# A gated-attention and soft-mixture kernel: PSUM halves as tiles of their own, halved first loads and y copies, and a new order of the first units and of the end

## Chip, cores and metric

One core of one Trainium2 chip runs the whole program. The metric is device time in microseconds (us) of one execution; lower is better. All data are fp32.

## The reference

For each of 4 batches and 8 heads a gated linear attention runs over 768 steps with head width 48; its output x (3072 rows of 384) goes through a soft mixture of 8 experts with 4 slots each.

```python
f = 1 / (1 + exp(-f_logit))
for t in range(768):
    state = f[:, :, t, :, None] * state + outer(k[:, :, t], v[:, :, t])
    y[:, :, t] = q[:, :, t] @ state
x = y as (3072, 384)
logits = x @ phi                                  # 3072 x 32
d = softmax of logits over the rows               # dispatch
slot_out[e] = relu((d.T @ x)[e] @ w1[e]) @ w2[e]  # 8 experts, hidden 1024
out = softmax of logits over the slots @ slot_out # combine
```

## The kernel before

**Units.** The sequence is cut into 6 chunks of 128 steps; a chunk of two batches is a unit (`u`, 12 units), with 16 (batch, head) pairs, two to a 128-partition block, in 8 blocks of 128 columns. For each unit the gates are turned into running sums by `d_exp`, `d_ln` (ScalarE) and `d_scan` (VectorE, line 191). `d_p` and `d_g` (ScalarE, lines 194 and 200) make the two exponentials of it, and `d_q` and `d_k` (lines 208 and 204, GpSimd but for unit 0) scale q and k with them. TensorE then makes the scores in two halves (`scores`, line 232), VectorE masks them (`s_mask`, line 235), TensorE transposes k (`kt`, copied by `kt_copy` on ScalarE), and y is summed in PSUM from the carried state (`inter`, line 272) and the masked scores (`intra`, line 281, two halves `w`). `kv` makes the unit's own contribution to the state, and `state_t` (line 257) and `state_2` (line 260), both on VectorE, carry it two units on. `y_copy` (ScalarE, line 293) takes y out of PSUM, `x_tr` transposes it back and `x_copy` takes one half out on ScalarE (line 311) and one on VectorE (line 313).

**Groups.** For each pair of units: `c_lg` (logits, line 325), `c_max`, `c_exp`, `c_tr` (transposes), `c_copy` (VectorE, line 353), `c_pin` (line 362) and `c_join` (VectorE, lines 366 and 367) keep the dispatch sum with a running maximum.

**End.** `up` (line 420, four times 24 matmuls), `turn` (line 426: transposes, then a masking multiply on VectorE), `down` (line 462, two column halves `h`), the combine softmax (`c_soft`, `c_soft2`, `c_ct`), `slot_out`, `slot_out2`, and for each half three `combine` and `store` steps, `flag` and `flag_2` compute a guard value that picks a slow path when the gates are too extreme (it does not run here).

**PSUM.** Four tiles of two banks each: `PA` holds the second scores half of unit 0, `x_tr`, `c_lg` and `c_pin`; `PB` holds y and `c_tr`; `PC` holds `kt` and `kv`; `PD` holds scores. Waits are set by the framework from the accesses to each tile.

**Order.** Every step is put on one list with a due time (`at`), unit `u` at `u * T` plus the offset of `OFF`; sorted, this gives each engine's program order, kept exactly. Units 0 and 1 have a list written out by hand. All loads and stores are issued by SyncE (SP), in the order of the list: the first loads in the list `first`, later ones by the offsets `lf`, `lk`, `lq`, `lv`, w1 and w2 pieces between them.

Of the kernel before, what the change touches and what calls it, by code (L numbers as in the profile page):

```python
# [31 lines left out]
def keep_order(tc):  # L32
# [16 lines left out]
    sc0=0, mask0=1.05, kt=1.1, ktok=1.95, sc1=2.85, mask1=3.95, inter=4.9, kv=5.4, intra0=5.7, st=6.2, s2=6.3, intra1=6.6, y=7.55,  # L49
# [8 lines left out]
def gla_soft_moe_kernel(ctx: ExitStack, tc: tile.TileContext, q, k, f, v, vd, phi, w1, w2, out):  # L58
# [65 lines left out]
    check = P([128, 8 * NU + NU + 2], "check")  # L124
# [12 lines left out]
    PA, PB, PC, PD = (pp.tile([128, 2, 512], F32, tag=n, name=n) for n in ("pa", "pb", "pc", "pd"))  # L137


    def consts_0():  # L140
        nc.gpsimd.memset(ones, 1.0)
        nc.vector.memset(again, 1.0)
        nc.vector.memset(again.rearrange("p (a t) -> p a t", t=L)[:, :, 0], 0.0)
        warm(20, PD[:, 1, :128])
        make_identity(nc, ident)
        nc.gpsimd.affine_select(mask, ones, pattern=[[1, L]], compare_op=ALU.is_ge, fill=0.0, base=0, channel_multiplier=-1)
        nc.vector.memset(PC, 0.0)
        nc.vector.memset(PB, 0.0)
# [73 lines left out]
    def SP(u, w):  # L222

        return PA if u == 0 and w else PD

    def scores(u, w):

        kq, qq = heads(R("k", u), L), heads(R("q", u), L)
        for p in range(4):
            for r in range(2):  # L230
                rs = slice(64 * r, 64 * r + D)
                nc.tensor.matmul(SP(u, w)[:, r, 128 * p : 128 * p + 128], kq[rs, 4 * w + p], qq[rs, 4 * w + p], start=True, stop=True)  # L232

    def s_mask(u, w):
        nc.vector.tensor_tensor(  # L235
            heads(R("sc", w), L), SP(u, w).rearrange("p r (a t) -> p (r a) t", t=L), mask.unsqueeze(1).broadcast_to([128, 8, L]), op=ALU.mult,
        )
# [25 lines left out]
    ys = heads(PB.rearrange("p w x -> p (w x)"), L)  # L263

    def inter(u):

        qq = heads(R("q", u), L)
        if u > 1:
            for p in range(4):
                for w, r in ((0, 0), (1, 1), (0, 1), (1, 0)):  # L270
                    a, o, rs = 4 * w + p, 64 * (r ^ w), slice(64 * r, 64 * r + D)
                    nc.tensor.matmul(  # L272
                        ys[o : o + D, a], heads(S0(u), D)[rs, a], qq[rs, a], start=p == 0, stop=False, skip_group_check=True,
                    )
# [22 lines left out]
    def y_last(u):  # L297
        t = xTs[u].rearrange("p n a t -> p n (a t)")
        nc.scalar.copy(t[:, 1, :256], PB[:, 1, :256])
        nc.vector.tensor_copy(t[:, 1, 256:], PB[:, 1, 256:])  # L300

    def x_tr(u):
        for w in range(2):
            for p in range(4):
                nc.tensor.transpose(PA[:, w, 128 * p : 128 * p + W], xTs[u][:W, w, p], ident[:W, :W])  # L305

    def x_copy(u, which=(0, 1)):
        x = xs[u].rearrange("p w (h d) -> p w h d", d=D)
        y = PA.rearrange("p w (h d) -> p w h d", d=64)[:, :, :, :D]
        if 0 in which:  # L310
            nc.scalar.copy(x[:, 0], y[:, 0])  # L311
        if 1 in which:
            nc.vector.tensor_copy(x[:, 1], y[:, 1])  # L313
# [41 lines left out]
    def pins(g):  # L355
        return PA[:, 1, :DM]
# [58 lines left out]
    UPB = [PA[:, 0], PA[:, 1], PC[:, 0], PC[:, 1]]  # L415
# [7 lines left out]
    def turn(j, hf):  # L423
        pt = PB[:, hf].rearrange("p (k m) -> p k m", k=4)
# [42 lines left out]
    def slot_out(h):  # L467
        hs_ = slice(HC * h, HC * h + HC)
        nc.vector.tensor_scalar(sob[:, hs_], PD[:, h, :HC], rzs, None, op0=ALU.mult)

    def slot_out2(h):

        hs_ = slice(HC * h, HC * h + HC)
        nc.tensor.matmul(PD[:, h, 256 : 256 + HC], same, sob[:, hs_], start=True, stop=True)
        nc.scalar.copy(s4[:, hs_], PD[:, h, 256 : 256 + HC])

    FIN = [[(PA, PC), (PB, PA), (PC, PB)], [(PA, PB), (PC, PD), (PA, PB)]]
    stage = [wr[:, 7 + 3 * h : 10 + 3 * h].rearrange("p a (n d) -> p (a n) d", d=HC).rearrange("p (v n) d -> p v n d", n=4) for h in range(NH)]

    def combine(h, y):  # L480

        hs_ = slice(HC * h, HC * h + HC)
        for x in range(2):
            for n in range(4):
                ns = slice(32 * n, 32 * n + 32)
                nc.tensor.matmul(FIN[h][y][n // 2][:, n % 2, HC * x : HC * x + HC], ct[ns, 2 * y + x], s4[ns, hs_], start=True, stop=True)
        for z in range(2):
            dst = stage[h][:, 2 * y : 2 * y + 2, 2 * z : 2 * z + 2].rearrange("p v n d -> p n v d")
            (nc.vector.tensor_copy if z else nc.scalar.copy)(dst, FIN[h][y][z][:, :, : 2 * HC].rearrange("p n (v d) -> p n v d", v=2))

# [244 lines left out]
```

## Time and profile before

| what | us |
|---|---|
| median of three runs | 175.89 (174.79 to 176.54) |
| the profiled execution, its own time | 177.31 |
| its span, first to last instruction | 175.6 |
| TensorE busy / VectorE / ScalarE / GpSimd | 145.7 / 105.1 / 91.7 / 54.5 |

A row of the timeline has the start in us, the duration in us, the engine (PE is TensorE, DVE VectorE, ACT ScalarE, POOL GpSimd, SPq SyncE's queue), the line, the operation, out and in tile, the shape and the number of instructions merged; in brackets stands the engine's idle time just before and what ended it. Releasers are inferred. TensorE's busy time contains pipelined work, and a slice of the page is a fortieth of the span, 4.39 us.

### The profile page before, as it was taken

The page shows a single profiled execution, that of the slowest core. Times are in us where ns is not written, and L with a number is a line of the kernel's source. Part 1 is how long each engine was busy: PE and PEld are TensorE (multiplying, and loading weights), DVE is VectorE, ACT ScalarE, POOL GpSimd, SP SyncE. Part 2 cuts the span into 40 slices and gives each one's busy share as a digit, 9 for nine tenths or more (in the row PEclk, how much of TensorE's full clock was granted, in tenths as well). Part 3 has the DMA queues.
Part 4 walks back from the last instruction along what each step waited for, and adds up shares of the span by engine and source line. Part 5 has one row for each costly group of instructions (what it writes and reads, how often), then busy time and mean ns, then how long its engine had stood idle before and what let it go on. Part 6 is the DMA issues. An engine that isn't in the chain of part 4 may idle for free.

```text
span 175.6 us, 5429 instructions
## 1 busy us (share of the span) xinstructions
PE 145.7 (83%) x2384; PEld 114.0 (65%) x2384; DVE 105.1 (60%) x143; ACT 91.7 (52%) x159; POOL 54.5 (31%) x43
## 2 busy tenths in 40 slices
PE   7679986799998989898989898999787997697600
PEld 7669875787886978697969786767422355464400
DVE  6786587629786959597859777581602327324600
ACT  4977794936868594949495865311311130223500
POOL 2007474741919091917372555400000000000000
PEclk9975999569999999999999999999999999999965
DMA  5999999969599999988899929999829990018790
GB/s 147 317 417 408 410 411 411 414 228 400 191 347 406 345 339 323 422 304 307 291 319 339 335 75 403 420 421 415 359 31 371 426 413 30 0 58 343 277 392 31
DMA packets 12848, 53.97 MB, mean 307 GB/s; under 512 B 1424, under 2 KB 1552, under 8 KB 12816
## 3 DMA queue, kind: packets, MB, share of 16 engines
q1 hardware_dynamic: 12816, 53.55, 79.5%
q8 instruction: 20, 0.33, 0.7%
q14 instruction: 12, 0.10, 0.2%
HBM read 48.82 MB, written 4.72 MB: 305 GB/s over the span
## 4 chain that ended last, share of the span: by engine, by line
PE 44%; DVE 28%; ACT 13%; issue 4%; DMA 4%; SPq 1%; DVEq 0%; ACTq 0%
DVE arena L191 11%; PE pb L272 6%; PE pc L250 5%; PE pd L462 4%; ACT arena L194 4%; DMA arena<-in_q_dram 4%; PE pd L232 4%; PE pa L420 3%; PE pc L420 3%; PE pa L325 3%; PE pa L362 3%; DVE arena L235 3%; PE pb L281 3%; DVE pc L257 3%; ACT arena L220 2%
## 5 line engine op out<-in xcount | busy, mean ns | idle before, releaser
L208 POOL TENSOR_TENSOR arena<-arena 128x1024 f32<-128x1024 f32 (+1 forms) x13 | 27.0, 2076 | 56.7 <-ACT arena L194 39.1
L232 PE MATMUL pd<-arena 48*128 48x128 f32 x368 | 27.7, 291 | 6.3 <-DVE arena L235 3.4
L235 DVE TENSOR_TENSOR arena<-pd,mask 128x1024 f32<-128x1024 f32 x23 | 27.8, 1210 | 4.0 <-PE pd L232 4.0
L191 DVE TENSOR_TENSOR_SCAN arena<-again,arena 128x1024 f32<-128x1024 f32 (+1 forms) x15 | 28.7, 1919 | 2.5 <-ACT arena L186 2.4
L232 PEld LDWEIGHTS pd<-arena 48*128 48x128 f32 x368 | 23.1, 193 | 10.6 <-DVE arena L235 5.5
L204 POOL TENSOR_TENSOR arena<-arena 128x1024 f32<-128x1024 f32 (+1 forms) x13 | 26.5, 2038 | 0.0
L281 PE MATMUL pb<-arena 128*48 128x128 f32 x384 | 24.4, 280 | 0.6 <-DVE arena L235 0.6
L281 PEld LDWEIGHTS pb<-arena 128*48 128x48 f32 x384 | 21.0, 126 | 1.6 <-DVE arena L235 0.9
L293 ACT COPY arena<-pb 128x1024 f32<-128x1024 f32 x11 | 11.1, 1011 | 14.5 <-PE pb L281 14.5
L194 ACT ACTIVATE arena<-arena 128x1024 f32<-128x1024 f32 (+1 forms) x15 | 13.3, 884 | 8.2 <-DVE arena L191 8.2
L183 ACT ACTIVATE arena<-arena 128x1024 f32<-128x1024 f32 (+1 forms) x14 | 13.1, 937 | 2.7 <-DMA arena<-in_f_dram 2.7
L272 PE MATMUL pb<-arena 48*48 48x128 f32 x320 | 11.8, 288 | 2.3 <-DVE el L353 2.3
L200 ACT ACTIVATE arena<-arena 128x1024 f32<-128x1024 f32 (+1 forms) x15 | 13.4, 892 | 0.3
L186 ACT ACTIVATE arena<-arena 128x1024 f32<-128x1024 f32 (+1 forms) x14 | 13.1, 936 | 0.4
L272 PEld LDWEIGHTS pb<-arena 48*48 48x48 f32 x320 | 9.1, 127 | 4.8 <-DVE el L353 2.9
L313 DVE COPY arena<-pa 128x384 f32<-128x384 f32 x12 | 6.6, 553 | 9.1 <-ACT arena L311 9.1
L427 DVE TENSOR_TENSOR arena<-pb,emask 128x512 f32<-128x512 f32 x4 | 2.8, 691 | 14.8 <-PE pb L426 14.8
L305 PE MATMUL pa<-ident,arena 112*128 112x112 f32 x96 | 11.3, 261 | 0.3 <-ACT arena L293 0.2
L217 PE MATMUL pc<-ident,arena 112*128 112x112 f32 x80 | 10.8, 280 | 0.5 <-POOL arena L204 0.5
L250 PEld LDWEIGHTS pc<-arena 128*48 128x48 f32 x320 | 9.1, 136 | 1.8 <-issue 1.7
L305 PEld LDWEIGHTS pa<-ident,arena 112*128 112x128 f32 x96 | 9.6, 141 | 0.8 <-ACT arena L293 0.6
L250 PE MATMUL pc<-arena 128*48 128x48 f32 x320 | 10.1, 221 | 0.0
(131 smaller groups left out, 201.4 us busy)
## 6 DMA issues: line engine op xcount, KB each, us to landing
wr<-in_w_dram SPq DMA_DIRECT2D x23, 768.0 KB, 8.6
arena<-in_w_dram SPq DMA_DIRECT2D x9, 768.0 KB, 8.0
arena<-in_k_dram SPq DMA_DIRECT2D x12, 512.0 KB, 6.4
arena<-in_q_dram SPq DMA_DIRECT2D x12, 512.0 KB, 7.2
arena<-in_f_dram SPq DMA_DIRECT2D x10, 512.0 KB, 7.0
arena<-in_v_dram SPq DMA_DIRECT2D x12, 384.0 KB, 7.3
out_dram<-wr SPq DMA_DIRECT2D x6, 768.0 KB, 4.2
arena<-in_f_dram SPq DMA_DIRECT2D x4, 256.0 KB, 5.1
```

Of the source, the lines that this page charges most:

```text
L183: nc.scalar.activation(cols(R("f", u), h), cols(R("f", u), h), AF.Exp, scale=-1.0, accum_out=a)
L191: nc.vector.tensor_tensor_scan(t, cols(again, h), t, 0.0, op0=ALU.mult, op1=ALU.add)
L194: nc.scalar.activation(cols(R("p", u), h), cols(R("f", u), h), AF.Exp, scale=-1.0)
L200: nc.scalar.activation(cols(G(u), h), cols(R("f", u), h), AF.Exp)
L204: (eng or nc.gpsimd).tensor_tensor(t, t, cols(G(u), h), op=ALU.mult)
L208: (eng or nc.gpsimd).tensor_tensor(t, t, cols(R("p", u), h), op=ALU.mult)
L232: nc.tensor.matmul(SP(u, w)[:, r, 128 * p : 128 * p + 128], kq[rs, 4 * w + p], qq[rs, 4 * w + p], start=True, stop=True)
L235: nc.vector.tensor_tensor(heads(R("sc", w), L), SP(u, w).rearrange("p r (a t) -> p (r a) t", t=L), mask.unsqueeze(1).broadcast_to([128, 8, ...
L250: nc.tensor.matmul(kvs[64 * r : 64 * r + D, a], kr[:, a, r], vb(u, a, r ^ a // 4), start=True, stop=True)
L272: nc.tensor.matmul(ys[o : o + D, a], heads(S0(u), D)[rs, a], qq[rs, a], start=p == 0, stop=False, skip_group_check=True,)
L281: nc.tensor.matmul(ys[o : o + D, 4 * w + p], vb(u, 4 * w + p, r ^ w), sc[:, r, p], start=u < 2 and p == 0, stop=p == 3, skip_group_check=True,
L305: nc.tensor.transpose(PA[:, w, 128 * p : 128 * p + W], xTs[u][:W, w, p], ident[:W, :W])
```

## The change

- **Tiles.** `PA` and `PB` become two tiles of one bank each (`PA[0]`, `PA[1]`, `PB[0]`, `PB[1]`); every user is rewritten to the bank it uses. `PC` and `PD` stay.
- **y in halves.** `y_copy` is two ScalarE copies of 128x512 (`y0` due after the first half of `intra`, `y1` after the second); for the last unit `y_last` (a split over ScalarE and VectorE) goes.
- **First loads.** k and q of unit 0 are loaded in column halves, q of unit 1 ahead of k, and v of unit 0 after both.
- **Order of units 0 to 3.** 28 instead of 20 `warm` matmuls (products of a tile of ones that nobody reads) before the first scores and 4 new ones before `kv` of unit 0; `s_mask` of unit 0 ahead of the scans of unit 1; second half of `d_q` of units 1 and 2 on VectorE; unit 2's gates partly in halves; `scan` of unit 3 after the first mask of unit 2 instead of ahead of it, `d_p` and `d_q` of unit 3 later.
- **End.** `up`, `turn`, `down`, `slot_out2`, `combine` get tiles of their own; `c_soft` moves ahead of the third `up`, `flag` into unit 11 and `flag_2` ahead of the fourth `up`; `combine` copies three tiles (one ScalarE copy of two banks, two VectorE copies of one).

```diff
-    PA, PB, PC, PD = (pp.tile([128, 2, 512], F32, tag=n, name=n) for n in ("pa", "pb", "pc", "pd"))
+    PA, PB = ([pp.tile([128, 512], F32, tag=f"{n}{w}", name=f"{n}{w}") for w in range(2)] for n in ("pa", "pb"))
+    PC, PD = (pp.tile([128, 2, 512], F32, tag=n, name=n) for n in ("pc", "pd"))
...
-        warm(20, PD[:, 1, :128])
+        warm(28, PD[:, 1, :128])
...
-    def y_copy(u):
-        t = xTs[u].rearrange("p n a t -> p n (a t)")
-        if u < NU - 1:
-            nc.scalar.copy(t, PB)
-        else:
-            nc.scalar.copy(t[:, 0], PB[:, 0])
+    def y_copy(u, which=(0, 1)):
+        for w in which:
+            nc.scalar.copy(xTs[u][:, w].rearrange("p a t -> p (a t)"), PB[w])
...
-    UPB = [PA[:, 0], PA[:, 1], PC[:, 0], PC[:, 1]]
+    UPB = [PA[0], PB[0], PA[0], PB[0]]
+    TURN = [[PB[1], PA[1]], [PB[1], PA[0]]]
+    DOWN = [PD[:, 0, :HC], PB[0][:, :HC]]
+    SUM = [PD[:, 1, 256 : 256 + HC], PA[0][:, 256 : 256 + HC]]
...
-    FIN = [[(PA, PC), (PB, PA), (PC, PB)], [(PA, PB), (PC, PD), (PA, PB)]]
+    FIN = [[(PC, PA[0], PA[1]), (PD, PB[1], PA[0]), (PC, PA[1], PB[1])], [(PC, PA[1], PB[1]), (PD, PA[0], PB[0]), (PC, PA[1], PB[1])]]
...
-        items = [(t_psi,), (c_exp, NV - 1, (1,)), (t_zs,), (up, 0, 0), (up, 0, 1), (c_tr, NV - 1, (1,)), (turn, 0, 0), (c_copy, NV - 1, (1,))]
-        items += [(up, 1, 0), (turn, 0, 1), (t_z,), (c_soft,), (up, 1, 1)]
+        items = [(t_psi,), (c_exp, NV - 1, (1,)), (t_zs,), (up, 0, 0), (up, 0, 1), (c_tr, NV - 1, (1,)), (c_copy, NV - 1, (1,)), (turn, 0, 0), (c_soft,)]
+        items += [(up, 1, 0), (turn, 0, 1), (t_z,), (flag_2,), (up, 1, 1)]
...
-    first = [(0, "f", 0), (0, "f", 1), (0, "k"), (0, "q"), (1, "f", 0), (1, "f", 1), (1, "k"), (0, "v"), (1, "q"), (2, "f"), (1, "v")]
+    first = [(0, "f", 0), (0, "f", 1), (0, "k", 0), (0, "q", 0), (0, "k", 1), (0, "q", 1), (1, "f", 0), (1, "f", 1), (1, "q"), (1, "k"), (0, "v"), (2, "f"), (1, "v")]
...
-        (d_exp, 1, 0), (d_ln, 1, 0), (d_exp, 1, 1), (d_ln, 1, 1), (d_pend, 0), (kt, 0), (d_scan, 1, 0), (s_mask, 0, 0), (d_p, 1, 0), (d_g, 1, 0),
-        (kt_copy, 0), (d_q, 1, 0), (d_k, 1, 0), (d_scan, 1, 1), (s_mask, 0, 1), (intra, 0, 0), (kv, 0), (d_p, 1, 1), (d_g, 1, 1), (d_q, 1, 1), (d_k, 1, 1),
-        (intra, 0, 1), (state_2, 0), (d_exp, 2), (y_copy, 0), (d_ln, 2), (d_pend, 1),
+        (d_exp, 1, 0), (d_ln, 1, 0), (d_exp, 1, 1), (d_ln, 1, 1), (d_pend, 0), (s_mask, 0, 0), (kt, 0), (d_scan, 1, 0), (d_scan, 1, 1), (s_mask, 0, 1),
+        (d_p, 1, 0), (d_g, 1, 0), (kt_copy, 0), (d_q, 1, 0), (d_k, 1, 0), (d_p, 1, 1), (d_g, 1, 1), (intra, 0, 0), (warm, 4, PD[:, 1, :128]), (kv, 0), (intra, 0, 1),
+        (d_q, 1, 1, V), (d_k, 1, 1), (state_2, 0), (d_exp, 2, 0), (d_ln, 2, 0), (y_copy, 0), (d_exp, 2, 1), (d_ln, 2, 1), (d_pend, 1),
...
-    for h in range(2):
-        for x, (fn, t) in enumerate(((d_scan, 1.5), (d_p, 2.9), (d_g, 3.0), (d_q, 2.95), (d_k, 3.05))):
-            at(T + t + 0.2 * h, fn, 2, h)
+    for t, fn, *args in (
+        (1.0, d_scan, 2, 0), (1.1, d_scan, 2, 1), (1.2, d_p, 2, 0), (1.25, d_g, 2, 0), (1.3, d_q, 2, 0), (1.35, d_k, 2, 0),
+        (2.0, d_p, 2, 1), (2.05, d_g, 2, 1), (2.1, d_k, 2, 1), (4.0, d_q, 2, 1, V),
+    ):
+        at(T + t, fn, *args)
+    early = {(1, "kv"): T + 6.0, (3, "scan"): 2 * T + 1.08, (3, "p"): 2 * T + 2.9, (3, "dq"): 2 * T + 2.95}
...
+    at((NU - 1) * T + 6.5, flag)
```

## Rows read from the trace of the kernel before

**Rows 1.** The page's slices: granted clock and DMA busy share, in tenths.

```profile
PEclk9975999569999999999999999999999999999965
DMA  5999999969599999988899929999829990018790
```

**Rows 2.** Timeline, the first 17 us.

```profile
1.06 6.23 PE L153 MATMUL pd<-ones 128*128 128x128 f32 x40 [1.06 <-POOL ones L141]
...
9.31 0.69 DVE L208 TENSOR_TENSOR arena<-arena 128x512 f32<-128x512 f32 x1 [0.57 <-DMA arena<-in_q_dram]
...
11.26 2.08 PE L232 MATMUL pa<-arena 48*128 48x128 f32 x16
...
14.22 1.63 POOL L208 TENSOR_TENSOR arena<-arena 128x512 f32<-128x512 f32 x1 [12.46 <-DMA arena<-in_q_dram]
...
14.96 1.95 PE L281 MATMUL pb<-arena 128*48 128x128 f32 x16
```

**Rows 3.** Timeline, 26 to 45 us, units 2 and 3.

```profile
26.24 1.16 PE L232 MATMUL pd<-arena 48*128 48x128 f32 x16
27.11 1.26 POOL L204 TENSOR_TENSOR arena<-arena 128x512 f32<-128x512 f32 x1
...
27.25 3.26 DVE L191 TENSOR_TENSOR_SCAN arena<-again,arena 128x1024 f32<-128x1024 f32 x1 [1.62 <-ACT arena L186]
...
30.44 1.19 DVE L235 TENSOR_TENSOR arena<-pd,mask 128x1024 f32<-128x1024 f32 x1
30.61 1.06 ACT L194 ACTIVATE arena<-arena 128x1024 f32<-128x1024 f32 x1 [2.49 <-DVE arena L191]
...
31.69 2.08 PE L232 MATMUL pd<-arena 48*128 48x128 f32 x16 [1.90 <-DVE arena L235]
...
39.88 2.28 DVE L191 TENSOR_TENSOR_SCAN arena<-again,arena 128x1024 f32<-128x1024 f32 x1
...
44.28 1.16 PE L232 MATMUL pd<-arena 48*128 48x128 f32 x16 [0.77 <-DVE arena L235]
```

**Rows 4.** Timeline of the loop, an even unit, in which a group ends.

```profile
71.38 0.56 DVE L313 COPY arena<-pa 128x384 f32<-128x384 f32 x1 [1.13 <-ACT arena L311]
...
71.99 0.85 PE L362 MATMUL pa<-arena,el 128*32 128x384 f32 x8 [0.53 <-DVE arena L313]
...
72.69 2.37 POOL L204 TENSOR_TENSOR arena<-arena 128x1024 f32<-128x1024 f32 x1
...
74.31 0.76 DVE L367 SCALAR_TENSOR_TENSOR sms<-sms,small 128x1 f32<-128x1 f32 x1
...
75.64 0.57 DVE L257 TENSOR_TENSOR pc<-pc,arena 128x384 f32<-128x384 f32 x1 [0.17 <-PE pc L250]
```

**Rows 5.** Timeline of the loop, a unit between two such.

```profile
100.60 1.09 PE L272 MATMUL pb<-arena 48*48 48x128 f32 x32 [0.76 <-DVE el L353]
100.95 2.38 POOL L204 TENSOR_TENSOR arena<-arena 128x1024 f32<-128x1024 f32 x1
...
103.67 2.28 DVE L191 TENSOR_TENSOR_SCAN arena<-again,arena 128x1024 f32<-128x1024 f32 x1
```

**Rows 6.** Timeline from the last unit to the last stores.

```profile
121.43 0.42 DVE L300 COPY arena<-pb 128x256 f32<-128x256 f32 x1 [3.05 <-ACT arena L299]
...
130.89 2.78 PE L420 MATMUL pa<-wr,et 128*32 128x512 f32 x24 [0.79 <-ACT arena L421]
...
135.41 2.78 PE L420 MATMUL pc<-wr,et 128*32 128x512 f32 x24 [1.05 <-DVE el L353]
...
145.83 0.63 PE L426 MATMUL pb<-ident,arena 128*128 128x128 f32 x4 [0.94 <-DVE arena L427]
...
150.76 0.55 PE L457 MATMUL pc<-ident,el 128*128 128x128 f32 x3 [0.57 <-ACT ct L458]
...
153.13 0.35 PE L462 MATMUL pd<-arena 128*32 128x192 f32 x1 [0.41 <-ACT s L475]
...
164.63 2.59 SPq L492 DMA_DIRECT2D out_dram<-wr  x3
```

More of the change, by code (lines that the diff above doesn't have):

```diff
@@ L147, in consts_0 @@
         nc.vector.memset(PC, 0.0)
-        nc.vector.memset(PB, 0.0)
+        for w in range(2):
+            nc.vector.memset(PB[w], 0.0)
     def warm(n, t=None):
@@ L220, in kt_copy @@
         nc.scalar.copy(heads(R("kt"), D), PC.rearrange("p b (a d) -> p (b a) d", d=64)[:, :, :D])
-    def SP(u, w):
-        return PA if u == 0 and w else PD
     def scores(u, w):
@@ L230, in scores @@
             for r in range(2):
-                rs = slice(64 * r, 64 * r + D)
-                nc.tensor.matmul(SP(u, w)[:, r, 128 * p : 128 * p + 128], kq[rs, 4 * w + p], qq[rs, 4 * w + p], start=True, stop=True)
+                rs, t = slice(64 * r, 64 * r + D), PD[:, r] if u or not w else PA[r]
+                nc.tensor.matmul(t[:, 128 * p : 128 * p + 128], kq[rs, 4 * w + p], qq[rs, 4 * w + p], start=True, stop=True)
     def s_mask(u, w):
-        nc.vector.tensor_tensor(
-            heads(R("sc", w), L), SP(u, w).rearrange("p r (a t) -> p (r a) t", t=L), mask.unsqueeze(1).broadcast_to([128, 8, L]), op=ALU.mult,
-        )
+        sc = heads(R("sc", w), L)
+        if u or not w:
+            parts = [(sc, PD.rearrange("p r (a t) -> p (r a) t", t=L))]
+        else:
+            parts = [(sc[:, 4 * r : 4 * r + 4], heads(PA[r], L)) for r in range(2)]
+        for dst, src in parts:
+            nc.vector.tensor_tensor(dst, src, mask.unsqueeze(1).broadcast_to(list(dst.shape)), op=ALU.mult)
     def vb(u, a, s):
@@ L260, in state_2 @@
         nc.vector.tensor_tensor(heads(S0(u + 2), D), kvs, pend[:, u].unsqueeze(2).broadcast_to([128, 8, D]), op=ALU.mult)
-    ys = heads(PB.rearrange("p w x -> p (w x)"), L)
+    ys = [heads(PB[w], L)[:, p] for w in range(2) for p in range(4)]
     def inter(u):
@@ L304, in x_tr @@
             for p in range(4):
-                nc.tensor.transpose(PA[:, w, 128 * p : 128 * p + W], xTs[u][:W, w, p], ident[:W, :W])
+                nc.tensor.transpose(PA[w][:, 128 * p : 128 * p + W], xTs[u][:W, w, p], ident[:W, :W])
     def x_copy(u, which=(0, 1)):
[L308 to L313, printed above, removed]
+        for w in which:
+            x, y = (heads(t, d)[:, :, :D] for t, d in ((xs[u][:, w], D), (PA[w], 64)))
+            (nc.vector.tensor_copy if w else nc.scalar.copy)(x, y)
     def lgs(g):
-        return (PA if g < NV - 1 else PC)[:, 0, :128]
+        return PA[0][:, :128] if g < NV - 1 else PC[:, 0, :128]
     def trs(g):
-        return PB[:, 0] if g < NV - 1 else PC[:, 1]
+        return PB[0] if g < NV - 1 else PC[:, 1]
     def c_lg(g):
@@ L423, in turn @@
     def turn(j, hf):
-        pt = PB[:, hf].rearrange("p (k m) -> p k m", k=4)
+        pt = TURN[j][hf].rearrange("p (k m) -> p k m", k=4)
         for kk in range(4):
@@ L482, in combine @@
         hs_ = slice(HC * h, HC * h + HC)
[L483 to L489, printed above, removed]
+        two, b2, b3 = FIN[h][y]
+        banks = [two[:, 0], two[:, 1], b2, b3]
+        for n2 in range(2):
+            for x in range(2):
+                for n in (n2, n2 + 2):
+                    ns = slice(32 * n, 32 * n + 32)
+                    nc.tensor.matmul(banks[n][:, HC * x : HC * x + HC], ct[ns, 2 * y + x], s4[ns, hs_], start=True, stop=True)
+        dst = stage[h][:, 2 * y : 2 * y + 2]
+        nc.scalar.copy(dst[:, :, :2].rearrange("p v n d -> p n v d"), two[:, :, : 2 * HC].rearrange("p n (v d) -> p n v d", v=2))
+        for n in (2, 3):
+            nc.vector.tensor_copy(dst[:, :, n], banks[n][:, : 2 * HC].rearrange("p (v d) -> p v d", v=2))
     def store(h, y):
@@ L575, in gla_soft_moe_kernel @@
             ("kt", kt), ("ktok", kt_copy), ("sc0", scores, 0), ("mask0", s_mask, 0), ("sc1", scores, 1), ("mask1", s_mask, 1),
-            ("kv", kv), ("st", state_t), ("s2", state_2), ("inter", inter), ("intra0", intra, 0), ("intra1", intra, 1), ("y", y_copy),
+            ("kv", kv), ("st", state_t), ("s2", state_2), ("inter", inter), ("intra0", intra, 0), ("y0", y_copy, (0,)), ("intra1", intra, 1), ("y1", y_copy, (1,)),
         ):
@@ L580, in gla_soft_moe_kernel @@
                 continue
-            at(z + o[key], fn, u, *args)
+            at(early.get((u, key), z + o[key]), fn, u, *args)
         if u < NU - 1:
```

39 lines of the change are left out of this document (18 added, 21 removed).

## The prediction, made before the changed kernel was run

> **What bounds the kernel now.** I read the page's slices first, then the chain of waits in order of time, then the timeline where the chain changes its pattern. The slices show two early stretches in which TensorE is granted its lower level (1.2 instead of 2.4 GHz), slice 3 and slices 7 and 8, and a transfer share near full up to about 100 us [rows 1]. The chain has four parts. (1) Loads of unit 0: VectorE waits for q until 9.31 [rows 2]. (2) Units 0 to 2: in unit 2 the scan of unit 3 stands ahead of unit 2's mask on VectorE, so the mask starts at 30.44 although its scores were ready at 27.4, and TensorE, which needs the scores tile back, idles 1.90 us and resumes at half clock (2.08 us for sixteen score products, 1.16 at full clock) [rows 3]. (3) The loop: scan, mask, second scores, `inter`, `kv`, state, next scan, with TensorE waiting 0.53 us behind `x_copy` in units with a group step and 0.76 us behind `c_copy` in the others [rows 4, 5]. (4) The end, where TensorE is the chain and waits for readers of another half of the tile that it wants to write [rows 6]; it closes with three stores issued from 164.63 on.
>
> **The kind of wait that is removed.** `x_copy` on VectorE (half 1 of `PA`) waits 1.13 us for ScalarE's copy of half 0 [rows 4], though both only read and touch different bytes. The third `up` (half 0 of `PC`) waits for a read of half 1 [rows 6]. So a tile of two banks is guarded as one thing. The PSUM page of the Trainium skill ("PSUM bank collisions raise a hardware error") wants engines kept apart within a bank, not across banks; by that rule these waits guard nothing, and tiles of one bank shed them without a new one.
>
> **Units 0 to 3.** The halves let the first k and q products start before 9.31, but that is not the gain: f of unit 1 keeps its place. v of unit 0 falls from eighth to eleventh load, to the point in the stream at which q of unit 1 was, and that landed just before 14.22. So `intra` of unit 0 starts at about 14.25 instead of 14.96 [rows 2]. The 8 added warm products (40 instructions took 6.23 us, so 16 at most 2.5) end by 9.8, before the second scores can start: nothing on the path, and they fill TensorE's idle time ahead of the scores. The 4 before `kv` cost at most 1.25 us on TensorE. The VectorE half of `d_q` of unit 1 queues `state_2`, the scan of unit 2 and the mask of unit 1 behind it, and may itself sit behind GpSimd (below). I give units 0 and 1 between 0 and 0.9 us, and take 0.6.
>
> Then unit 2: scores at 25.6 (26.24 before), done 26.8; mask 1.19 to 28.0; scan of unit 3 from 28.05. In the old order it took 3.26 instead of 2.28 because GpSimd's product ran until 28.37 [rows 3]; now GpSimd has nothing in that stretch: done 30.35. The second scores then start at 28.6 instead of 31.69 (mask done, and an estimated 0.6 for `x_tr` of unit 1, which stands ahead of them and waits for the new y copies), with the clock up. What is late next: `d_p` of unit 3 (1.06) ends at 31.45, then two GpSimd products of 2.37 [rows 3, 4] end at 36.2, and only then can the scores of unit 3 and, by the lock, the scan of unit 4 start. From that scan's start to the second scores of unit 3 were 39.88 to 44.28, 4.4 us [rows 3]; so these start at 40.6: **3.7 us earlier**. With nothing gained in units 0 and 1 it is 3.0, with all 4.0.
>
> **Loop.** The waits removed suggest 0.53 and 0.76 us per unit, but another end is close behind. `c_join`'s short instruction L367 lasts 0.76 us and ends at 75.07, when GpSimd's L204 ends (75.06); behind it stand `c_max` and the state's L257 at 75.64, only 0.17 after it could have run [rows 4]. GpSimd's end hangs on the scan, not on `x_copy`, so a unit with a group step gains about 0.15. In the others TensorE gets to `kv` 0.76 earlier and the scan could start at 102.9 instead of 103.67, but GpSimd's L204 runs until 103.33 [rows 5]: about 0.3 us. From the second scores of unit 3 on there are three units of the second kind whose wait is on the chain, four of the first (the first of them has no L367 and may gain 0.45), and one wait of 0.3 in unit 11: 0.9 + 0.6 + 0.3 = **1.8 us**. Bounds: 0, and 3 x 0.76 + 4 x 0.53 = 4.4 if the stretched instruction is not a lock. The SBUF page of the Trainium skill ("Who interferes with whom") has this as an exclusive lock of a port pair between VectorE and GpSimd, whoever issues first holding it for its whole instruction. The trace agrees by the two ends 0.01 us apart. By that rule the loop gives 1.8, without it 4.4. The second y half costs ScalarE one more start per unit; ScalarE is busy half the span and waits for `intra` there, so nothing.
>
> **Last unit and end.** y of unit 11 ended with a copy of 0.42 that waited for ScalarE's to end; now one half-copy is left for the end: **0.45 us**, about that copy (bounds 0 and 0.85, two such). Then each wait of rows 6 goes, since the new `UPB`, `TURN`, `DOWN` and `c_ct` tiles alternate: 0.79 (second `up`), 1.05 (third), 0.94 (fourth `turn`), 0.57 (second `c_ct`), 0.41 (`down` behind `slot_out2`'s copy) = **3.8 us** [rows 6]. They add up because TensorE is the chain between them. The one place where VectorE sets it is `c_soft2`; its input, the fourth `turn`, comes earlier by the first three, and the flag instructions now stand ahead. Bounds 2.5 to 4.2. `combine` has two VectorE copies instead of one; the first can start when half of the products are done, so 0. The last three stores run one behind the other from 164.63; that start moves with the sum. Late w2 loads start when the first `up` is done, so they move along.
>
> **Sum.** 3.7 + 1.8 + 0.45 + 3.8 = 9.7 us. The profiled execution (177.31, span 175.6) comes to 167.6, span 165.9. It lies 1.4 above the median, and I put the sum against the median: 175.89 - 9.7 = **166.2 us**, own range 164.5 to 167.8.
>
> **The rivals.**
> - *No lock in the way.* The loop gives 4.4: 163.6. For it: TensorE's idle time is seen directly. Against: L367's end. 13%.
> - *The clock falls in the new order.* Before, it fell after TensorE had idled from 7.3 (warm products done) to 10.0 (first q product done) and again around the 1.90 us before 31.69; it stayed through the 0.77 us before 44.28 [rows 1 to 3]. In the new order I estimate 1.6 us idle before 14.25 (k's transposes done, v not there) and 1.4 us before 36.2 (unit 2 done, GpSimd not): between these ends. A fall makes 3.9 us of work on the path cost up to 0.8 of itself more (2.08 against 1.16): 1.6 to 3.1 us, 167.8 to 169.3. 23%.
> - *Transfers set the loop.* Share mostly 0.8 and more there [rows 1], so the 1.8 may not come: 168.0. Against: the chain shows no load behind the first q. 6%.
> - *The waits stay*, because the framework guards something else than tiles, so loop and end give nothing: 175.89 - 3.7 - 0.45 = 171.7. Against: the third `up` waits for the other half of a tile and nothing else. 8%.
> - *Slower.* A clock fall that lasts: with 9.7 + 1.8 us to lose and 0.8 us lost per us of path work at the lower level, it takes over 14 us of such work more than the two stretches of before. The place would be 11 to 45 us. Against: from slice 9 on the old loop, with more idle time, keeps the full level [rows 1]. Over 177.7. 3%.
>
> **How the numbers follow.** Forecast 42%, rivals 13, 23, 6, 8, 3; 5% for something unnamed, shared between both sides. The range 163 to 170.5 takes in the forecast, the first three rivals and leaves the other two and the unnamed, some 16%. About 1% is what a measurement of this kernel can tell from no change. Forecast and four rivals are faster by more than that, with half of the unnamed less a residue: 0.92; same 0.05; slower 0.03.
>
> **What would show it.** Right: L313's copy no longer waits for ScalarE's; second scores of unit 2 near 28.6 at 1.16 us; second scores of unit 3 near 40.6; the loop's units shorter by 0.15 and 0.3 us; L367 or the scan still ending or starting where GpSimd ends; first `up` to first store of the second half about 3.8 us shorter. Wrong: a slice with a low granted clock before 45 us, a new wait of TensorE in units 0 to 3, or a loop with the same period.

## The result, and the profile after

The changed kernel takes **164.86 us** (164.71 to 165.38, four runs) against 175.7 (174.79 to 176.54): a ratio of 0.939, 95% interval 0.934 to 0.944. The forecast was 166.2, its own range 164.5 to 167.8. A kernel's time below is the median of its executions within 1.5% of the fastest.

The page's slices of the changed kernel, granted clock and transfer share, show one fall of the clock (slices 8 and 9, counted from 0) ahead of the end, where the kernel before had two (2 and 3, 7 and 8) [rows 1]:

```profile
PEclk9999999986999999999999999999999999999955
DMA  5999999999999999998999919999947996048690
```

To see where the time came from, cut both profiled executions at the same steps. Two of the cuts are not among the rows ahead of the prediction; the timeline of the kernel before has them (the second scores of unit 11, the first `up`; between them TensorE's wait behind `c_copy` in unit 11):

```profile
115.30 1.16 PE L232 MATMUL pd<-arena 48*128 48x128 f32 x16
...
116.73 0.85 PE L362 MATMUL pa<-arena,el 128*32 128x384 f32 x8 [0.27 <-DVE el L353]
...
127.31 2.78 PE L420 MATMUL pa<-wr,et 128*32 128x512 f32 x24 [0.39 <-DVE small L430]
```

| stretch | before | after | gain | forecast |
|---|---|---|---|---|
| start to the second scores of unit 3 | 44.28 | 39.37 | 4.91 | 3.7 |
| to the second scores of unit 11 | 71.02 | 68.63 | 2.39 | 1.5 |
| to the first `up` | 12.01 | 11.37 | 0.64 | 0.75 |
| to the first of the last three stores | 37.32 | 32.95 | 4.37 | 3.8 |
| to the end of the span | 10.97 | 10.68 | 0.29 | 0 |
| span | 175.6 | 163.0 | 12.6 | 9.7 |

The forecast's loop term of 1.8 holds 0.3 for the wait in unit 11 at 116.73, which lies behind the second cut, so it stands in two rows. All gains but that of the third row are larger than forecast, yet the medians differ by 10.8. The difference lies in the profiled execution of before, which was 1.6 us above its median (177.31 to 175.7): its mean granted clock was 0.940, where 39 executions of that kernel beside the experiments had 0.954 to 0.975 and spans of 171.8 to 174.5, and only one other had 0.940. I put these 1.6 us in the first row: with the old start in the changed kernel (below) and no fall in slices 2 and 3, unit 2's scores start at 24.68 instead of 26.24. That is argued and not shown, since that kernel has the bank tiles as well.

The timeline of the changed kernel, TensorE, units 2 and 3 (their four score steps, and `kt` and `x_tr` of unit 3):

```profile
24.14 1.16 PE L231 MATMUL pd<-arena 48*128 48x128 f32 x16
...
27.11 1.16 PE L231 MATMUL pd<-arena 48*128 48x128 f32 x16
...
34.74 1.16 PE L231 MATMUL pd<-arena 48*128 48x128 f32 x16 [1.83 <-POOL arena L207]
35.84 1.75 PE L220 MATMUL pc<-ident,arena 112*128 112x112 f32 x8
37.38 1.70 PE L300 MATMUL pa<-ident,arena 112*128 112x112 f32 x8
...
39.37 1.16 PE L231 MATMUL pd<-arena 48*128 48x128 f32 x16
```

Unit 2's first scores start at 24.14 (26.24 before), its second at 27.11 without a wait and at 1.16 us, the full level (31.69 and 2.08 before, [rows 3]). Then TensorE waits 1.83 us for GpSimd's k product of unit 3, and right behind it the granted clock falls: `kt` takes 1.75 and `x_tr` 1.70 instead of the 0.99 and 0.93 us of other units.

The same timeline, VectorE, ScalarE and GpSimd in the loop (first `x_copy`, L305, of one unit; then a group step):

```profile
46.97 0.56 DVE L305 COPY arena<-pa 128x384 f32<-128x384 f32 x1
...
47.62 0.48 ACT L305 COPY arena<-pa 128x384 f32<-128x384 f32 x1
...
66.83 2.38 POOL L207 TENSOR_TENSOR arena<-arena 128x1024 f32<-128x1024 f32 x1
67.30 1.93 DVE L359 SCALAR_TENSOR_TENSOR sms<-sms,small 128x1 f32<-128x1 f32 x1
69.14 0.28 DVE L327 TENSOR_REDUCE small<-pa 128x1 f32<-128x128 f32 x1
```

VectorE copies its half of `x` before ScalarE has begun the other: the 1.13 us of [rows 4] is gone. What is next in line is the short instruction on one element per partition (L359, the L367 of [rows 4]): it begins at 67.30 beside GpSimd's product and both end at 69.2. It was 0.76 us in [rows 4] and is 1.93 here, because it comes earlier under the same product. A pair of units takes 17.72 us (scores at 64.42 and 82.14) instead of 18.41.

The same timeline, the end:

```profile
119.37 2.78 PE L415 MATMUL pa<-wr,et 128*32 128x512 f32 x24 [0.39 <-DVE et L405]
121.97 2.76 PE L415 MATMUL pb<-wr,et 128*32 128x512 f32 x24
...
125.35 2.78 PE L415 MATMUL pa<-wr,et 128*32 128x512 f32 x24
...
128.90 2.78 PE L415 MATMUL pb<-wr,et 128*32 128x512 f32 x24
...
134.71 0.60 PE L421 MATMUL pa<-ident,arena 128*128 128x128 f32 x4
...
135.72 2.81 PE L458 MATMUL pd<-arena 128*32 128x192 f32 x64 [0.41 <-DVE arena L422]
...
139.10 0.49 PE L453 MATMUL pa<-ident,el 128*128 128x128 f32 x3
...
152.32 2.23 SPq L493 DMA_DIRECT2D out_dram<-wr  x3
```

The `up`s but the first, the fourth `turn` (134.71) and the second `c_ct` (139.10) have no bracket: these waits of [rows 6] are gone. One of 0.41 us is new: the `down` at 135.72 waits for VectorE's multiply of the third `turn`, for which the fourth `turn` waited before.

### The profile page after: what moved, and what is told of

It is laid out like the page before. It is cut to its first block, busy times and chain, and to the rows that moved or that the text cites. A ratio compares the mean times of both kernels' runs of the same rounds, so it can differ in the third digit from the quotient of the medians.

```text
span 163.0 us, 5511 instructions
## 1 busy us (share of the span) xinstructions
PE 143.0 (88%) x2408; PEld 113.6 (70%) x2408; DVE 112.6 (69%) x152; ACT 92.6 (57%) x173; POOL 53.4 (33%) x41
## 4 chain that ended last, share of the span: by engine, by line
## 5 line engine op out<-in xcount | busy, mean ns | idle before, releaser
L211 POOL TENSOR_TENSOR arena<-arena 128x1024 f32<-128x1024 f32 (+1 forms) x11 | 25.0, 2270 | 50.5 <-ACT arena L197 36.1
L194 DVE TENSOR_TENSOR_SCAN arena<-again,arena 128x1024 f32<-128x1024 f32 (+1 forms) x15 | 30.4, 2036 | 1.7 <-ACT arena L189 1.5
L231 PE MATMUL pd<-arena 48*128 48x128 f32 x368 | 26.7, 285 | 5.2 <-DVE arena L240 3.1
L207 POOL TENSOR_TENSOR arena<-arena 128x1024 f32<-128x1024 f32 (+1 forms) x13 | 27.3, 2104 | 0.0
L295 ACT COPY arena<-pb 128x512 f32<-128x512 f32 x24 | 13.5, 586 | 6.5 <-PE pb L284 6.2
L300 PE MATMUL pa<-ident,arena 112*128 112x112 f32 x96 | 12.3, 273 | 0.0
L275 PE MATMUL pb<-arena 48*48 48x128 f32 x320 | 10.9, 274 | 0.0
L156 PE MATMUL pd<-ones 128*128 128x128 f32 x64 | 9.6, 320 | 1.1 <-POOL ones L143 1.1
L156 PEld LDWEIGHTS pd<-ones 128*128 128x128 f32 x64 | 9.2, 233 | 1.2 <-POOL ones L143 1.1
L220 PEld LDWEIGHTS pc<-ident,arena 112*128 112x128 f32 x80 | 8.4, 149 | 1.2
L253 PE MATMUL pc<-arena 128*48 128x48 f32 x320 | 9.2, 210 | 0.0
```

Of the source, the lines that this page charges most:

```text
L156: nc.tensor.matmul(PC[:, 1, 384:512] if t is None else t, ones, ones, start=True, stop=True)
L194: nc.vector.tensor_tensor_scan(t, cols(again, h), t, 0.0, op0=ALU.mult, op1=ALU.add)
L207: (eng or nc.gpsimd).tensor_tensor(t, t, cols(G(u), h), op=ALU.mult)
L211: (eng or nc.gpsimd).tensor_tensor(t, t, cols(R("p", u), h), op=ALU.mult)
L220: nc.tensor.transpose(PC[:, a // 4, 128 * (a % 4) : 128 * (a % 4) + W], kq[:W, a], ident[:W, :W])
L231: nc.tensor.matmul(t[:, 128 * p : 128 * p + 128], kq[rs, 4 * w + p], qq[rs, 4 * w + p], start=True, stop=True)
```

## Experiments

Two theories stood against each other. *Tiles*: the bank tiles free the loop and the end, up to GpSimd's lock on VectorE. *Order*: the new start and the new order of short steps bring the gain, and the tiles little. All edits below are against the changed kernel unless said otherwise. The interval of the changed kernel's ratio to the kernel before is 0.934 to 0.944; only the whole y copy, the halved k product and the end's tiles have an interval clear of it, so a smaller difference of medians counts only as far as a trace shows it.

**Two-bank tiles again, y still in halves.**

```diff
-    PA, PB = ([pp.tile([128, 512], F32, tag=f"{n}{w}", name=f"{n}{w}") for w in range(2)] for n in ("pa", "pb"))
+    PA2, PB2 = (pp.tile([128, 2, 512], F32, tag=n, name=n) for n in ("pa", "pb"))
+    PA, PB = [PA2[:, 0], PA2[:, 1]], [PB2[:, 0], PB2[:, 1]]
```

> The changed kernel (164.9 us) with one thing undone: PA and PB are again one tile of two banks each, and every user takes the same bank of it as before. If a tile is guarded as one thing whatever bank is touched, the VectorE copy of x_copy waits for ScalarE's copy again (1.1 us, as in the kernel before), the loop goes back from 17.7 to about 18.4 us for two units, and in the end the second up, the turns and the combines wait for readers of the other half: 168.5 to 171 us. If the waits of before had another cause, nothing changes: 164.9.

178.41 us in a single execution (the profiled one took 182.19): at least 13.5 us above the changed kernel, slower than the kernel before, and far beyond the expected 168.5 to 171. The waits of TensorE in the profile of this kernel (what waited, for whom; us in total, times, longest) and then those of VectorE name the cause:

```profile
PE pb L285 <- ACT arena L296: 10.7, 11, 2.8
```

```profile
DVE arena L306 <- ACT arena L306: 8.5, 10, 1.9
```

The second half of `intra` writes the other bank while ScalarE copies the first half of y out; in one tile that is a wait, 11 times. The y copy in halves puts ScalarE's copy between the two halves of `intra`. With bank tiles TensorE has no such wait: in the changed kernel ScalarE copies a first half from 52.67 to 53.26, while `intra` runs from 51.58 to 53.50 without a gap.

**The same, with y in one copy as before.**

```diff
-        for w in which:
-            nc.scalar.copy(xTs[u][:, w].rearrange("p a t -> p (a t)"), PB[w])
+        if 1 in which:
+            nc.scalar.copy(xTs[u].rearrange("p n a t -> p n (a t)"), PB2)
```

> As the kernel with PA and PB as tiles of two banks (182.2 us), but y is copied by one ScalarE instruction after both halves, as before. In that kernel the second half of intra waited 0.7 us in each unit for ScalarE's copy of the first half. If that is the cause of its long loop, the loop goes back to the 18.4 us per two units of the kernel before and the start gets shorter too: 0.7 us in each of 11 units, 173.5 to 175.5 us. If the loop is long for another reason, about 182.

174.38 us, ratio to before 0.996 (0.991 to 1.001). Everything else of the change, loads, order, end, gives no measurable gain without bank tiles. The loop is back at 71.0 us (second scores at 41.00 and 112.00), the old 71.02. *Order* alone does not hold; with all the rest in place, bank tiles and halved y copies are worth 9.5 us. What the bank tiles give in the old order throughout was not run.

**The start as before, bank tiles kept.** First loads, list of the first units, due times and 20 warm products of the kernel before.

```diff
-        warm(28, PD[:, 1, :128])
+        warm(20, PD[:, 1, :128])
...
-    early = {(1, "kv"): T + 6.0, (3, "scan"): 2 * T + 1.08, (3, "p"): 2 * T + 2.9, (3, "dq"): 2 * T + 2.95}
+    early = {}
```

> The changed kernel with the start of the kernel before: its order of first loads (whole k and q of unit 0), its list for units 0 and 1, its due times for units 2 and 3, 20 warm products. Tiles of one bank, y in halves and the new end stay. If the start is worth the 4.9 us by which the changed kernel's second scores of unit 3 came earlier in the profiles, or rather the 4.9 less the about 1.5 us by which the kernel before's profiled execution lay above its median: 168.3 to 169.8 us. If most of that gain came from the tiles, 166 to 167.

167.09 us (165.87 to 167.16): by the medians the new start is worth 2.2 us, less than expected (the intervals of the two ratios, 0.941 to 0.956 and 0.934 to 0.944, overlap). Unit 1's first scores start at 17.22 here, at 18.91 in the profiled execution of before and at 17.02 in the changed kernel. Its slices show no fall of the clock before slice 7, where the profiled execution of before had one in slices 2 and 3 [rows 1].

**Only the scan of unit 3 in its old place.**

```diff
-    early = {(1, "kv"): T + 6.0, (3, "scan"): 2 * T + 1.08, (3, "p"): 2 * T + 2.9, (3, "dq"): 2 * T + 2.95}
+    early = {(1, "kv"): T + 6.0}
```

> The changed kernel with the early due times of unit 3's scan, d_p and d_q taken back, so that the scan of unit 3 stands ahead of unit 2's first mask on VectorE again. If this order was what made TensorE wait in unit 2, its second scores start about 2 to 3 us later than 27.1 and the clock may fall there; but unit 3's gates come earlier than in the changed kernel, so part is given back when the scores of unit 3 wait for GpSimd: 165.5 to 168 us. If the gain of units 0 to 3 came from the other edits, 164.9.

165.88 us, 1.0 above the changed kernel. The timeline of this kernel, TensorE, second scores of unit 2 and of unit 3:

```profile
29.14 2.08 PE L231 MATMUL pd<-arena 48*128 48x128 f32 x16 [1.88 <-DVE arena L240]
...
40.30 1.16 PE L231 MATMUL pd<-arena 48*128 48x128 f32 x16 [0.77 <-DVE arena L240]
```

The wait of [rows 3] is back (1.88 for 1.90), and the half clock with it. This one move is close to half of the start's 2.2.

**Only the first loads as before.**

```diff
-    first = [(0, "f", 0), (0, "f", 1), (0, "k", 0), (0, "q", 0), (0, "k", 1), (0, "q", 1), (1, "f", 0), (1, "f", 1), (1, "q"), (1, "k"), (0, "v"), (2, "f"), (1, "v")]
+    first = [(0, "f", 0), (0, "f", 1), (0, "k"), (0, "q"), (1, "f", 0), (1, "f", 1), (1, "k"), (0, "v"), (1, "q"), (2, "f"), (1, "v")]
```

> The changed kernel with the old order of the first loads alone: k and q of unit 0 whole, v of unit 0 ahead of q of unit 1. The first q then comes at about 9.3 instead of before 8 us, the first scores about 0.8 us later, v of unit 0 earlier. If the first products set the pace of units 0 and 1: 165.3 to 166 us. If v of unit 0 did, 164 to 164.9.

165.15 us (164.94 to 165.4) against 164.86 (164.71 to 165.38): 0.3, and the runs overlap, so no effect of these loads by themselves is shown.

**The warm products as before (20, none ahead of `kv`).**

```diff
-        warm(28, PD[:, 1, :128])
+        warm(20, PD[:, 1, :128])
...
-        ... (intra, 0, 0), (warm, 4, PD[:, 1, :128]), (kv, 0), (intra, 0, 1),
+        ... (intra, 0, 0), (kv, 0), (intra, 0, 1),
```

> The changed kernel with the old 20 warm products before the first scores and without the 4 before kv of unit 0. If they only fill time that TensorE has to wait anyway and keep the granted clock up, the clock falls in the first 20 us as in the kernel before and the products there take up to 1.8 times as long: 1 to 3 us more, 165.9 to 168 us. If the clock stays up without them, 164.0 to 164.9, as the 4 products stand on TensorE's path (1.2 us) and go.

164.01 us (163.54 to 164.73): 0.85 below the changed kernel's median. The timelines of the changed kernel and then of this one, TensorE, warm products and first scores, show where:

```profile
1.06 8.44 PE L156 MATMUL pd<-ones 128*128 128x128 f32 x56 [1.06 <-POOL ones L143]
9.43 1.16 PE L231 MATMUL pd<-arena 48*128 48x128 f32 x16
```

```profile
1.06 6.99 PE L156 MATMUL pd<-ones 128*128 128x128 f32 x40 [1.06 <-POOL ones L143]
8.54 1.16 PE L231 MATMUL pd<-arena 48*128 48x128 f32 x16 [0.50 <-DVE arena L211]
```

In the changed kernel the first scores stand behind 56 warm instructions until 9.43, though VectorE's first half of q was ready at 8.57 (7.89 and 0.68). The 0.89 us is passed on: unit 0's mask at 9.82 instead of 10.71, unit 2's first scan half at 16.69 instead of 17.57, its first scores at 23.26 instead of 24.14. As VectorE carries this delay from the mask on, the traces put the cost on the eight products at the start and not on the four ahead of `kv` (the second alternative of the expectation had it the other way round); no run takes out one of the two alone.

**No VectorE instruction with two SBUF inputs in the group step.** The running sum goes to ScalarE; the running maximum takes its old value as a per-partition pointer.

```diff
-            nc.vector.tensor_tensor(nm(g), nm(g - 1), bmx, op=ALU.min)
+            nc.vector.tensor_scalar(nm(g), bmx, nm(g - 1), None, op0=ALU.min)
...
-            nc.vector.scalar_tensor_tensor(sms[:, 0:1], sms[:, 0:1], alpha, sms[:, 1:2], op0=ALU.mult, op1=ALU.add)
+            nc.scalar.activation(sms[:, 0:1], sms[:, 0:1], AF.Identity, bias=sms[:, 1:2], scale=alpha)
```

> The changed kernel with the two short VectorE instructions of a group that have two operands in SBUF taken out of GpSimd's way: the running sum of c_join is one ScalarE instruction, the running maximum of c_max takes the old maximum as a scalar operand. If VectorE is blocked by GpSimd's products only in instructions with two SBUF tensors, the 1.9 us instruction is gone, the state update of the three group units starts at the end of kv, about 0.3 us earlier each: 163.9 to 164.4 us. If the running maximum with its scalar operand is blocked as well, or if the block was not what set the state update, 164.9.

164.17 us; the loop from the second scores of unit 3 to those of unit 11 is 67.90 instead of 68.63, a pair of units 17.35 instead of 17.72. Its timeline, VectorE and GpSimd in the same group step:

```profile
66.48 2.38 POOL L207 TENSOR_TENSOR arena<-arena 128x1024 f32<-128x1024 f32 x1
67.04 0.29 DVE L327 TENSOR_REDUCE small<-pa 128x1 f32<-128x128 f32 x1
67.36 0.21 DVE L329 TENSOR_SCALAR nmx<-small,nmx 128x1 f32<-128x1 f32 x1
...
69.90 2.28 DVE L194 TENSOR_TENSOR_SCAN arena<-again,arena 128x1024 f32<-128x1024 f32 x1
```

The pointer form runs in 0.21 us in the middle of GpSimd's product; nothing is stretched, and the scan starts 0.70 earlier than at 70.60; 0.34 of that was there at this unit's second scores (64.08 instead of 64.42), the rest is what this group step gives.

**Half of GpSimd's k product left out from unit 3 on.**

```diff
-        t = cols(R("k", u), h)
-        (eng or nc.gpsimd).tensor_tensor(t, t, cols(G(u), h), op=ALU.mult)
+        t, g = cols(R("k", u), h), cols(G(u), h)
+        if u > 2:
+            t, g = t[:, :512], g[:, :512]
+        (eng or nc.gpsimd).tensor_tensor(t, t, g, op=ALU.mult)
```

> The changed kernel with half of GpSimd's product for k left out from unit 3 on (the second half of k stays unscaled, so that part of the computation is missing). GpSimd ends 1.1 us earlier in each unit. If its products hold VectorE back, the scan that follows is no longer stretched, the stretched running sum gets short, and the loop goes to the pace of TensorE's own work: some 0.6 us per two units, 2 us in all; and the scores of unit 3, which wait for k, and the scan of unit 4 start about 1.2 us earlier: 161.5 to 162.5 us. If VectorE's long instructions have another reason, only the 1.2 us of unit 3 come: 163.7 us.

161.95 us; loop 67.22, a pair 17.26, unit 3's first scores at 33.20 instead of 34.74. The timeline of this kernel, GpSimd and VectorE:

```profile
64.56 1.29 POOL L209 TENSOR_TENSOR arena<-arena 128x512 f32<-128x512 f32 x1
65.03 0.84 DVE L361 SCALAR_TENSOR_TENSOR sms<-sms,small 128x1 f32<-128x1 f32 x1
67.98 2.28 DVE L194 TENSOR_TENSOR_SCAN arena<-again,arena 128x1024 f32<-128x1024 f32 x1
```

With a product of 1.29 us (64.56 to 65.85) the short instruction ends at 65.87: again where GpSimd's does. Both experiments show the same limit of the loop from two sides.

**Six warm products ahead of unit 3's first scores.**

```diff
+    at(3 * T - 0.05, warm, 6, PD[:, 1, :128])
```

> The changed kernel with six more warm products just before unit 3's first scores, where TensorE stood idle for 1.83 us (before 34.74) and the granted clock fell at about 35.8. Theory (the idle time lets the clock fall): no fall in slices 8 and 9, kt and x_tr of that stretch near 1.0 and 0.93 instead of 1.75 and 1.70, second scores of unit 3 near 39.0, median 164.3 to 164.6. Rival (the fall has nothing to do with that idle time): the median stays within 164.7 to 165.3, and a fall, if there is one, stands elsewhere or in the same place.

164.5 us (163.88 to 164.75) against 164.86 (164.71 to 165.38); the ratio to before is 0.939 for both, so a gain is not shown. The timeline of this kernel, TensorE:

```profile
32.97 1.60 PE L156 MATMUL pd<-ones 128*128 128x128 f32 x12
35.00 1.16 PE L231 MATMUL pd<-arena 48*128 48x128 f32 x16 [0.43 <-POOL arena L207]
36.09 0.99 PE L220 MATMUL pc<-ident,arena 112*128 112x112 f32 x8
36.92 0.93 PE L300 MATMUL pa<-ident,arena 112*128 112x112 f32 x8
...
39.21 1.16 PE L231 MATMUL pd<-arena 48*128 48x128 f32 x16 [1.15 <-DVE arena L240]
```

The clock keeps its level (`kt` 0.99, `x_tr` 0.93), yet the second scores come only 0.16 earlier: they wait 1.15 us for VectorE's mask. The fall had been nearly hidden. Nor does the length of the idle time alone decide: the next kernel has the same 1.83 us and no fall.

**The two useful edits together: old warm products, no short two-input instruction.** Both diffs as above.

> The changed kernel with the two edits together that each gave something alone: c_lg's running sum as one ScalarE activation and c_max with its running value as a pointer (no VectorE instruction with two SBUF inputs there), and the warm products as before (20 at the start, none ahead of kv). Theory (they act in different stretches, loop and units 0 to 3, and add): 0.6 + 0.85 below 164.86, so 163.2 to 163.6; second scores of unit 3 near 38.1, the pair of units near 17.35. Rival (what the earlier start gains is lost at the loop's end, or the other way): 164.0 as with the warm products alone.

163.09 us (162.81 to 163.92), ratio to before 0.933 (0.930 to 0.937): its median is below both kernels' and near the sum of the two (164.86 - 0.85 - 0.69 = 163.32); the intervals of the three ratios overlap. Its timeline, TensorE, unit 3:

```profile
33.94 1.16 PE L231 MATMUL pd<-arena 48*128 48x128 f32 x16 [1.83 <-POOL arena L207]
35.04 0.99 PE L220 MATMUL pc<-ident,arena 112*128 112x112 f32 x8
35.86 0.93 PE L300 MATMUL pa<-ident,arena 112*128 112x112 f32 x8
```

**And unit 3's GpSimd products in halves, the constants' copies moved away from its mask.** The edit to the kernel with the two useful edits; `const_same` holds the four copies.

```diff
-        ... (d_k, 0, 1, V), (d_q, 0, 1, V), (scores, 0, 1),
+        ... (d_k, 0, 1, V), (d_q, 0, 1, V), (const_same,), (scores, 0, 1),
...
+            if u == 3 and key in ("dk", "dq"):
+                continue
...
+    for x, (fn, h, t) in enumerate(((d_q, 0, 2.95), (d_k, 0, 4.4), (d_k, 1, 4.41), (d_q, 1, 4.42))):
+        at(2 * T + t, fn, 3, h)
```

> As e12_both, and unit 3's GpSimd products in halves in the order first half of q, both of k, second half of q, with the four copies that repeat the constants for both halves moved into VectorE's idle time of the start. Theory (before 34.74 TensorE waited 1.83 us for GpSimd's k product, which stood behind whole products and the scan's lock): unit 3's first scores 1.5 to 2 earlier, its second 1.1 earlier, median about 1 us below e12_both, near 162.3. Rival (four halves of about 1.27 cost GpSimd more than two whole of 2.37, and the scan of unit 4 behind them sets the second scores): no gain over e12_both.

162.71 us (162.47 to 163.96); the interval of its ratio, 0.927 to 0.935, overlaps the last one's, so a gain over it isn't shown. Unit 3's scores come 1.08 and 0.86 us earlier (32.86, 37.30), but unit 4's second only 0.13 (45.71 instead of 45.84). This kernel's timeline, VectorE's scan of unit 4, GpSimd's last half product, ScalarE's next exponential:

```profile
33.48 2.55 DVE L195 TENSOR_TENSOR_SCAN arena<-again,arena 128x1024 f32<-128x1024 f32 x1 [1.10 <-ACT arena L190]
...
33.84 3.26 POOL L212 TENSOR_TENSOR arena<-arena 128x512 f32<-128x512 f32 x1
...
36.43 1.06 ACT L198 ACTIVATE arena<-arena 128x1024 f32<-128x1024 f32 x1 [1.57 <-DVE arena L195]
```

Here VectorE's scan was first, and GpSimd's half product took 3.26 us instead of some 1.3. The scan ends at 36.03, as in the kernel before this one (32.56 and 3.48), so unit 4's exponential starts at 36.43 as there (36.44). It was 0.93 us shorter but began 0.92 later, because the start had become slower: unit 2's first scores come at 24.28 instead of 23.35. The copies found no idle time there (unit 0's mask starts at 10.54 instead of 9.91), and in this profile the granted clock, after TensorE had idled 1.66 us before 13.49, is 0.75 from 12 to 16 us and 0.82 from 16 to 20. Unit 3's mask starts where the scan ends (35.96); the copies, 0.89 us, no longer stand between, and that is its second scores' gain of 0.86. What the halves alone are worth stays open.

**The end's tiles as before in three places.**

```diff
-    UPB = [PA[0], PB[0], PA[0], PB[0]]
-    TURN = [[PB[1], PA[1]], [PB[1], PA[0]]]
+    UPB = [PA[0], PA[1], PC[:, 0], PC[:, 1]]
+    TURN = [[PB[0], PB[1]], [PB[0], PB[1]]]
...
-        t = PA[1] if h else PC[:, 0]
+        t = PC[:, h]
```

> The changed kernel with the tiles of the end as they were in three places: the third and fourth up on the two halves of PC, the turns on the two halves of PB, both c_ct on the two halves of PC. Units 0 to 11 keep their tiles of one bank. Theory (each wait of the end was one on the other half of a two-bank tile; on PB, whose halves are two tiles now, the fourth turn's 0.94 stays away, on PC the third up's 1.05 and the second c_ct's 0.57 come back): first up to first of the last three stores 1.0 to 1.6 longer than 32.95, median 165.9 to 166.5. Rival (the end's 4.4 came from the tiles of its own, not from one bank each, so the fourth turn's wait comes back too): 167.0 to 167.5. Other rival (the new order of the short steps there hides them): 164.7 to 165.2.

166.65 us, 1.8 above the changed kernel; the stretch from the first `up` (119.56) to the first of the last three stores (154.54) is 34.98 instead of 32.95. Its timeline, TensorE:

```profile
119.56 5.36 PE L415 MATMUL pa<-wr,et 128*32 128x512 f32 x48 [0.39 <-DVE et L405]
...
125.56 2.78 PE L415 MATMUL pc<-wr,et 128*32 128x512 f32 x24
...
129.69 0.27 PE L504 MATMUL pc<-ident,gok 128*1 128x128 f32 x1 [0.63 <-ACT arena L416]
130.33 2.78 PE L415 MATMUL pc<-wr,et 128*32 128x512 f32 x24 [0.37 <-DVE gok L505]
...
135.64 1.09 PE L421 MATMUL pb<-ident,arena 128*128 128x128 f32 x8
...
141.27 0.55 PE L453 MATMUL pc<-ident,el 128*128 128x128 f32 x3 [0.57 <-ACT ct L454]
```

On the two halves of `PA`, now two tiles, the first two `up`s run in one go (119.56, 48 products), and on those of `PB` the third and fourth `turn` (135.64, eight transposes). On `PC`, still one tile, the second `c_ct` waits 0.57 as in [rows 6]. The third `up` does not wait, since `c_copy` now comes earlier, but `flag_2`, which writes the other half of the third `up`'s tile, waits 0.63 for its reader, and the fourth `up` 0.37 for the reader of `flag_2`. So, in this order of steps, about 2 us of the end's gain needs the new tiles in these three places, while the second `up`'s 0.79 and the fourth `turn`'s 0.94 stay away by the bank tiles alone. `DOWN`, `SUM` and `FIN` kept their new tiles, so what those give is not shown.

## Why the prediction was right

- **The kind of wait.** "So a tile of two banks is guarded as one thing" holds: the two-bank tiles bring the waits back, between two engines that only read (VectorE for ScalarE in `x_copy`, 8.5 us) as between reader and writer. The Trainium skill (page "PSUM — Partial Sum Buffer", section "PSUM bank collisions raise a hardware error") asks for engines to be kept apart within a bank; the traces agree that a wait between banks can be left out (the y copy from 52.67 beside `intra`, above). That wait costs 13.5 us at its worst (178.41 against 164.86).
- **Units 0 to 3** (3.7). By the profiles 4.9, of which 2.1 stand in units 0 and 1 (24.14 instead of 26.24; `intra` of unit 0 starts at 13.19 where about 14.25 was expected), for which 0.6 was taken. In medians the whole start is worth 2.2, and without the bank tiles it brings nothing measurable (174.38), where the prediction's rival of the waits that stay left it the full 3.7: the start's gain, too, hung on the tiles, which the prediction did not say. The mis-sized step is the choice of the profiled execution as the usual case: [rows 1] showed a fall in slice 3, and its price was neither taken out of the sum nor named as something that other executions do not have. That the sum was set against the median did not remedy this, since the term itself stayed.
- **"The 8 added warm products ... nothing on the path"** failed. They cost 0.85 by the medians (0.89 at the first scores): the text held them against the second scores, but the first scores stand behind them in TensorE's order, and their inputs were now ready at 8.57, by the halved loads of the same change (with the old loads the first scores start at 10.39). "The 4 before `kv`" did cost nothing by the traces.
- **What is late next in unit 3**, GpSimd's two products, was right: 1.83 us of waiting before 34.74. The text had 36.2 and 40.6 for the scores of unit 3; 34.74 and 39.37 came, 1.2 to 1.5 us earlier, about as much as unit 2 began earlier (24.14 for 25.6).
- **Loop** (1.5 up to the second scores of unit 11): 2.4. The limit was named rightly. The short instructions with two inputs now fall under GpSimd's product (L359 for 1.93 us, in another unit L329 for 1.51), and scans do too (2.60 us at 60.65 instead of 2.28); taking the short ones away gives 0.7 us more and halving the product 1.4. A pair gained 0.69 where 0.45 (0.15 and 0.3) was forecast. The Trainium skill (page "SBUF — State Buffer", section "Who interferes with whom") calls the port pair that VectorE and GpSimd share an exclusive lock, has a VectorE instruction with two SBUF inputs contend for it, and lets the order of issue decide who waits; the traces agree both ways, with 1.93 us for 0.21 on VectorE and 3.26 for about 1.3 on GpSimd. The rival without a lock, 4.4, is out.
- **Last unit and end** (0.75 with the wait of unit 11, and 3.8): 0.64 and 4.37, all named waits gone and one of 0.41 new. That they add up along TensorE was right. The bound 4.2 was passed by 0.2; the moved flag instructions, put at nothing, are a candidate, which no run tells apart.
- **The clock rival** came in part: one fall, at the second of the two places named (before unit 3's scores). The prediction also named a low slice before 45 us as a sign of being wrong. The fall's price was put at 1.6 to 3.1 us; by the traces it was 0.2 to 0.4, because VectorE's mask held the second scores anyway.
- **The total.** 9.7 was forecast and 10.8 measured: loop, last unit, end and stores gave 1.6 us more than their terms, in the start the medians gave 1.5 less, and the remaining 1.0 lies within the spread of the runs of before (171.8 to 174.5 us of span). That the total came within 1.1 us is in part luck: the start was forecast too large and the rest too small.

## What to carry to other kernels

Where two engines touch different banks of one PSUM tile, make the banks tiles of their own before reordering anything: here the reordering gave nothing measurable without that and both together 10.8 us, and splitting a copy without splitting its tile cost some 4 us (178.41 against 174.38). Filler work for TensorE has to end before the first real product can start, counted after the change's own gains. Before sizing a gain from one profile, look whether its clock falls are those of the usual execution.

## What the runs showed that was not expected

- A VectorE instruction on one element per partition can last 1.93 us under GpSimd's product. The running maximum lasted 1.51 us under one, and 0.21 with its old value as a pointer.
- The granted clock falls at different places in nearly the same code: here in slices 8 and 9 (after 1.83 us of idle time), in slice 7 with the old scan order (1.88), in none with the old warm products (2.13 us before 13.96, 1.85 before 33.87), with the old loads (1.82 before 35.70) or with the two useful edits together (1.83 before 33.94). Idle time of this length therefore came with a fall in some executions and without in others; what decides stays open.
